# Attention scores of three batches as three rounded products, in four chunks of 112 query rows

## The chip, the cores and the metric

The kernel runs on one core of a Trainium2 chip. The metric is the time of one execution on the device, in microseconds (us). A profiled execution of the same program gives the rows shown below; its times count from the first instruction. Engines: PE is TensorE (matmuls and transposes), DVE is VectorE, ACT is ScalarE, POOL is GpSimd, SP is the engine whose queue issues nearly all transfers.

## The reference

Attention whose heads are mixed before and after the softmax, and then a gated feed-forward layer over all tokens. Batch 4, 12 heads, 448 positions, head size 64; 1792 tokens of 768, hidden size 1536; all in float32.

```python
scores = scale * np.matmul(q, k.transpose(0, 1, 3, 2))
scores = np.einsum('bhij,hg->bgij', scores, w_pre)
scores = scores - np.max(scores, axis=-1, keepdims=True)
attn = np.exp(scores)
attn = attn / (np.sum(attn, axis=-1, keepdims=True) + 1e-09)
attn = np.einsum('bhij,hg->bgij', attn, w_post)
attn_out = np.matmul(attn, v)
g = x @ w_gate            # x: attn_out as 1792 rows of 768
out = (g * sigmoid(g) * (x @ w_val)) @ w_out
```

The change touches the first line alone: the scores of batches 1, 2 and 3.

## The kernel before

**Two stages.** For about the first 410 us the attention of four batches runs, and then the feed-forward layer to the end. The change lies in the first.

**Scores.** q and k are loaded as rows (`load_q`, `load_k`), turned by PE transposes into PSUM (`qprep`: three transposes, half a chunk of queries; `kprep`: four transposes, the keys of a pair of heads), and copied to SBUF (`qcopy` and `kcopy`, tiles `qt` and `kk`). `qk` then multiplies: a group is one pair of heads `p` and one chunk `c` of query rows; head 0 of the pair lies on partitions 0 to 63, head 1 on 64 to 127, so that a group is two products of 64 rows deep, 448 columns wide, one in each half of the array, each into a PSUM bank of its own. Both are float32. `qkcopy` moves the banks to SBUF (`stg`; on ACT or DVE by the parity of the group), and `store` writes them to DRAM (`s_all`), where the scores of all heads of one query row stand together. For batches 1 to 3 chunk 0 has 64 rows (three groups of two pairs, so four products each) and chunks 1 to 3 have 128 (six groups each): 21 groups a batch.

**Steps.** The rest of the attention goes in 23 steps `u` a batch, each of 20 query rows (two tiles of ten). In a step: `gather` reads scores from DRAM (tile `rs`, five buffers, issued two and a half steps ahead), `pre` mixes heads on PE into two PSUM banks, `top` takes row maxima on DVE, `expo` exponentiates on ACT (`e`; reading the banks of `pre` a last time), `norm` and a POOL instruction scale the second mixing's weights, `post` mixes again on PE (for the step before the last two), `mixed` copies that on ACT (`attnT`). In steps 14 to 19 of a batch and 2 to 7 of the next PE also does `av`, attention times values (`values` copies it out); I call these long steps. The others, 8 to 13 and 20 to 1, are short steps. `pre` has two PSUM banks in all, so that `pre` of a step needs that both `expo` of the step before are done.

**Order.** Nothing is scheduled at run time. `at(key, fn)` gives each piece of work a key, and all engines issue by rising key; a step is two units of key long. Within a step `pre` has 0.5, `qk` 0.55, `top` 0.6, `kprep` 0.65, `qprep` 0.66, `qkcopy` 0.7 (1.1 on ACT for even groups), `kcopy` 0.8, `qcopy` 0.81, `expo` 0.95, `post` of an earlier step 1.2, `av` 1.3, `store` 1.4. The scores of a batch are worked out ahead, in steps 14 to 22 of the batch before and 0 to 11 of its own; its k is turned in steps 10 to 15 of the batch before, its chunk 0 of q in steps 11 and 12 there, the halves of chunks 1 to 3 in steps 16, 19, 21 (at its end), 2, 5 and 8. `BACK` sets where this begins.

Of the kernel before, what the change touches and what calls it, by code (L numbers as in the profile page):

```python
# [24 lines left out]
def talking_heads_moe_kernel(ctx, tc, q, k, v, w_pre, w_post, w_gate, w_val, w_out, out):  # L25
# [128 lines left out]
    def scored(c):  # L154
        return P if c else PART

    def row(c):
        return PART + (c - 1) * P if c else 0
# [17 lines left out]
    def load_q(b, c, eng=nc.sync):  # L176
        m = scored(c)
# [1 line left out]
        eng.dma_start(out=qn[b, c][:m], in_=q[b, :, row(c):row(c) + m, :].rearrange("h p d -> p h d"))
# [847 lines left out]
```

## Time and profile before

| | |
|---|---|
| time, median of 3 runs | 944.69 us (943.44 to 947.01) |
| profiled execution, its own time | 941.46 us |
| its span, first to last instruction | 939.7 us |
| mean granted TensorE clock | 0.985 |
| busy over the span | PE 96%, DVE 69%, ACT 46%, POOL 23% |
| the chain that ended last | PE 81%, transfers 9%, DVE 5%, ACT 3% |
| score products (`qk`) on that chain | 6% |

The table's shares are means over two stages that have different limits, so they only say that PE matters most. Matmuls overlap, and a matmul that waits inside the engine counts as busy: whether PE sets the pace in a stretch is read from the order of time there.

### The profile page before, as it was taken

To read this page: it belongs to the slowest core of one execution; us is meant where nothing else is said; L and a number is where in the kernel's file an instruction comes from. 1 tells how busy PE (TensorE), PEld (TensorE's weight loads), DVE (VectorE), ACT (ScalarE), POOL (GpSimd) and SP (SyncE) were. 2 spreads that over 40 slices of the span, in tenths; PEclk is the share of its full clock that TensorE was granted. 3 is DMA by queue.
4 is the path that set the end of the run, shared out by engine and by line. 5 is a ranking of instruction groups with operands and counts; after the bars stand their busy time and mean duration, and the time that the engine had idled before them with its cause. 6 is when DMAs were issued, how large, how long until landed. Compare 5 with 4: busy or idle time off the path is not lost.

```text
span 939.7 us, 27013 instructions
## 1 busy us (share of the span) xinstructions
PE 900.0 (96%) x11276; PEld 717.1 (76%) x11276; DVE 644.0 (69%) x1169; ACT 429.7 (46%) x1006; POOL 219.1 (23%) x291
## 2 busy tenths in 40 slices
PE   8779999899989999899999999999999999999998
PEld 5445655565546565678999999999998999999998
DVE  3556565566655756666999999999849999973210
ACT  2465676567655767553333333333234444431210
POOL 2111111121211111103334443444133332310000
PEclk9799999999989999999999999999999999999999
DMA  8999888998897679523644445476531222211311
GB/s 157 299 284 297 276 285 251 298 290 272 261 324 232 202 273 310 182 95 104 197 152 151 152 151 173 157 268 233 195 113 46 68 68 68 68 51 51 125 40 40
DMA packets 142130, 170.48 MB, mean 181 GB/s; under 512 B 56472, under 2 KB 117432, under 8 KB 142008
## 3 DMA queue, kind: packets, MB, share of 16 engines
q1 hardware_dynamic: 138536, 167.27, 55.9%
q10 hardware_dynamic: 3408, 1.48, 0.8%
q8 instruction: 89, 1.46, 0.7%
q14 instruction: 33, 0.27, 0.1%
q0 software_dynamic: 64, 0.00, 0.0%
HBM read 105.71 MB, written 63.02 MB: 180 GB/s over the span
## 4 chain that ended last, share of the span: by engine, by line
PE 81%; DMA 9%; DVE 5%; ACT 3%; issue 2%; SPq 1%; ACTq 0%; DVEq 0%
PE pre L319 7%; PE av L405 7%; PE dn L842 6%; PE dn L843 6%; PE dn L844 6%; PE post L363 6%; DMA rs<-s_all 6%; PE qk L270 6%; PE p L752 5%; PE p L755 5%; PE p L753 5%; PE upv L808 3%; PE upv L809 3%; PE upv L812 3%; PE upg L812 3%; PE upg L808 3%
## 5 line engine op out<-in xcount | busy, mean ns | idle before, releaser
L336 ACT ACTIVATE e<-pre,st 128x448 f32<-128x448 f32 x180 | 112.6, 630 | 110.8 <-DVE st L330 110.8
L330 DVE TENSOR_REDUCE st<-pre 128x1 f32<-128x448 f32 x180 | 104.0, 618 | 79.2 <-PE pre L319 76.2
L842 PE MATMUL dn<-whi,gh 128*128 128x256 f32 x504 | 141.1, 280 | 1.3 <-DVE u L759 1.3
L844 PE MATMUL dn<-whi,gl 128*128 128x256 f32 x504 | 141.0, 280 | 0.0
L843 PE MATMUL dn<-wlo,gh 128*128 128x256 f32 x504 | 141.0, 280 | 0.0
L347 POOL TENSOR_SCALAR rw<-w_post_gs,st 128x60 f32<-128x60 f32 x180 | 54.3, 317 | 337.9 <-DVE st L344 322.5
L656 POOL TENSOR_SCALAR mag<-mag 128x768 f32<-128x768 f32 x33 | 98.6, 2988 | 145.7 <-ACT mag L654 145.7
L363 PEld LDWEIGHTS post<-rw,e 60*64 60x64 f32 x5040 | 89.5, 138 | 44.9 <-issue 29.7
L319 PE MATMUL pre<-rs,w_pre_blocks 64*64 64x448 f32 (+1 forms) x720 | 103.4, 565 | 21.2 <-DMA rs<-s_all 18.1
L363 PE MATMUL post<-rw,e 60*64 60x60 f32 x5040 | 102.0, 225 | 5.5 <-issue 4.4
L378 ACT ACTIVATE attnT<-post 128x420 f32<-128x420 f32 (+1 forms) x192 | 91.1, 541 | 15.8 <-PE post L363 15.3
L842 PEld LDWEIGHTS dn<-whi,gh 128*128 128x128 f32 x504 | 94.7, 188 | 1.6 <-DVE u L759 1.5
L843 PEld LDWEIGHTS dn<-wlo,gh 128*128 128x128 f32 x504 | 94.7, 188 | 0.0
L844 PEld LDWEIGHTS dn<-whi,gl 128*128 128x128 f32 x504 | 94.7, 188 | 0.0
L405 PE MATMUL av<-attnT,vn 128*64 128x120 f32 (+9 forms) x1728 | 89.4, 262 | 2.7 <-issue 0.9
L270 PE MATMUL qk<-kk,qt 64*128 64x448 f32 (+1 forms) x432 | 88.2, 584 | 0.4 <-DVE qt L248 0.4
L405 PEld LDWEIGHTS av<-attnT,vn 128*64 128x64 f32 (+1 forms) x1728 | 70.8, 136 | 15.3 <-issue 6.4
L279 DVE COPY stg<-qk 128x448 f32<-128x448 f32 x120 | 70.9, 616 | 6.6 <-PE qk L270 6.2
L270 PEld LDWEIGHTS qk<-kk,qt 64*128 64x128 f32 (+1 forms) x432 | 26.9, 165 | 53.7 <-issue 29.7
L684 DVE TENSOR_TENSOR wlo<-w,whi 128x768 fp32r<-128x768 f32 x48 | 45.6, 951 | 29.4 <-ACT whi L688 29.2
L688 ACT ACTIVATE whi<-w 128x768 fp32r<-128x768 f32 x48 | 40.0, 837 | 32.0 <-PE dn L844 21.4
L798 ACT ACTIVATE gh<-m 128x448 fp32r<-128x448 f32 x36 | 20.9, 580 | 71.6 <-DVE m L823 63.4
(120 smaller groups left out, 1672.2 us busy)
## 6 DMA issues: line engine op xcount, KB each, us to landing
rs<-s_all SPq DMA_DIRECT2D x88, 448.0 KB, 5.6
s_all<-stg SPq DMA_DIRECT2D x60, 448.0 KB, 4.9
w_d<-w SPq DMA_DIRECT2D x36, 384.0 KB, 2.7
w<-w_d SPq DMA_DIRECT2D x36, 384.0 KB, 3.4
s_all<-stg SPq DMA_DIRECT2D x45, 224.0 KB, 4.5
raw<-in_moe_w_gate_dram SPq DMA_DIRECT2D x12, 768.0 KB, 4.8
raw<-in_moe_w_val_dram SPq DMA_DIRECT2D x12, 768.0 KB, 6.0
raw<-in_moe_w_out_dram SPq DMA_DIRECT2D x12, 768.0 KB, 5.0
```

The lines of the kernel that those rows point to most:

```text
L270: nc.tensor.matmul(pt[x][i * m:(i + 1) * m], qt[b, c][hs, p, o:o + m], kk[b, p][hs], start=True, stop=True)
L279: nc.vector.tensor_copy(stg[b, c, g][:, x], pt)
L319: nc.tensor.matmul(pt[r][x * HB:(x + 1) * HB], wpre[i], xs[i, x], start=True, stop=True)
L330: nc.vector.tensor_reduce(sts[b, u][:, 0, r:r + 1], pts[b, t], axis=AX.X, op=ALU.max, negate=True)
L336: nc.scalar.activation(e, pts.pop((b, t)), AF.Exp, bias=st[:, 0, r:r + 1], scale=1.0, accum_out=st[:, 1, r:r + 1])
L363: nc.tensor.matmul(ats[b, u][y][o * HB:(o + 1) * HB, to, :m], et[b, t][i, c * P + x * HB:c * P + (x + 1) * HB], rw[b, t][i, :, :m], start= ...
L378: nc.scalar.activation(attnT[:part, i, n0:n1, y * HS:y * HS + m], pt[:part, n0:n1, :m], AF.Copy)
L405: nc.tensor.matmul(o, vn[b][part, h, c], a, start=(c == 0 and x == 0), stop=(c == NC - 1 and x == 2 - m))
L656: eng.tensor_scalar(mag, mag, f32_of(0x38000000), f32_of(0x47EFFFFF), op0=ALU.max, op1=ALU.min)
L842: nc.tensor.matmul(pt, gh, hi, start=opens, stop=False)
L843: nc.tensor.matmul(pt, gh, lo, start=False, stop=False)
L844: nc.tensor.matmul(pt, gl, hi, start=False, stop=closes)
```

## The change

Batches 1 to 3 now split what comes out of the transposes: ACT writes a rounded copy (`hi`, type float32r) and DVE the difference (`lo`, float32r). A score is then three products, hi x hi, hi x lo (k) and lo x hi (q), each one instruction, summed in the same PSUM bank. Chunks have 112 query rows for these batches, so 4 x 6 = 24 groups a batch, each a pair of heads. The keys of a batch are two tiles of all pairs (`xb0`, `xa0` and so on), shared in turn with the tiles of the attention's output. Batch 0 computes as before.

The order moves. `BACK` is 13: everything of a batch's scores begins one step earlier. Groups stand in steps 13 to 22 and 0 to 12, chunk 3 starting one step sooner (`behind` -1), so that step 7 has two groups and every other step one. k is turned in steps 9 to 14, chunk 0 of q in 10 and 11, the other halves in 18, 21, 1, 4, 6 and 9. The diff, cut to its core:

```diff
+    def parted(t, hi, lo):
+        nc.scalar.activation(hi, t, AF.Copy)
+        nc.vector.tensor_tensor(lo, t, hi.bitcast(F32), op=ALU.subtract)
+
     def kcopy(b, p):
-        kk[b, p] = kkp.tile([P, S], F32, tag="kk", name=f"kk_{b}_{p}")
-        if b == 0 and p % 2 == 0:
-            nc.scalar.activation(kk[b, p], trs.pop((b, p)), AF.Copy)
-        else:
-            nc.vector.tensor_copy(kk[b, p], trs.pop((b, p)))
...
+        tr, to = trs.pop((b, p)), [t[:, p] for t in kk[b]]
+        if b:
+            parted(tr, *to)
...
     def qcopy(b, c, g):
-        m = scored(c)
-        nc.vector.tensor_copy(
-            qt[b, c][:, g * (NPAIR // 2):(g + 1) * (NPAIR // 2), :m], qtrs.pop((b, c, g))[:, :, :m]
-        )
+        m = scored(b, c)
+        ps_ = slice(g * (NPAIR // 2), (g + 1) * (NPAIR // 2))
+        tr, to = qtrs.pop((b, c, g))[:, :, :m], [t[:, ps_, :m] for t in qt[b, c]]
+        if b:
+            parted(tr, *to)
+        else:
+            nc.vector.tensor_copy(to[0], tr)
...
-        for i, p in enumerate(pairs):
-            for x in range(2):
-                hs = slice(x * D, (x + 1) * D)
-                nc.tensor.matmul(
-                    pt[x][i * m:(i + 1) * m], qt[b, c][hs, p, o:o + m], kk[b, p][hs], start=True, stop=True
-                )
+        terms = ((0, 0), (0, 1), (1, 0)) if b else ((0, 0),)
+        for j, (u, v) in enumerate(terms):
+            for i, p in enumerate(pairs):
+                for x in range(2):
+                    hs = slice(x * D, (x + 1) * D)
+                    a, w = qt[b, c][u][hs, p, o:o + m], kk[b][v][hs, p]
+                    nc.tensor.matmul(
+                        pt[x][i * m:(i + 1) * m], a, w, start=j == 0, stop=j == len(terms) - 1
+                    )
...
-    BACK = 14
+    BACK = 13
...
-            behind = 0 if b else 2
+            behind = 3 if b == 0 else -1 if c == NC - 1 else 0
```

On PE, in step 10 of batch 1, this stood after `pre` before the change (`qk_1_3_4` is batch 1, chunk 3, pair 4; the last number of a name is its bank or its buffer):

```order
L270 MATMUL qk_1_3_4_0_2731<-kk_1_4_1262,qt_1_3_2337 128x448
L270 MATMUL qk_1_3_4_1_2732<-kk_1_4_1262,qt_1_3_2337 128x448
L224 MATMUL ktr_2_0_2739<-ident_99,kn_2_0_2519 128x128 x3
L224 MATMUL ktr_2_0_2739<-ident_99,kl_2_2517 128x64
L363 MATMUL post_1_8_0_2757<-rw_1_16_2649,e_1_16_2614 64x60 x2
```

and this stands there now (`qt0` is hi of q, `qt1` lo; `kk_1_xb0` is hi of k, `kk_1_xa0` lo):

```order
L285 MATMUL qk_1_3_3_0_2839<-kk_1_xb0_893,qt0_1_3_2495 112x448
L285 MATMUL qk_1_3_3_1_2840<-kk_1_xb0_893,qt0_1_3_2495 112x448
L285 MATMUL qk_1_3_3_0_2839<-kk_1_xa0_894,qt0_1_3_2495 112x448
L285 MATMUL qk_1_3_3_1_2840<-kk_1_xa0_894,qt0_1_3_2495 112x448
L285 MATMUL qk_1_3_3_0_2839<-kk_1_xb0_893,qt1_1_3_2496 112x448
L285 MATMUL qk_1_3_3_1_2840<-kk_1_xb0_893,qt1_1_3_2496 112x448
L220 MATMUL ktr_2_1_2851<-ident_96,kn_2_1_2608 128x128 x3
L220 MATMUL ktr_2_1_2851<-ident_96,kl_2_2502 128x64
L250 MATMUL qtr_2_0_0_2858<-ident_96,qn_2_0_2475 128x112 x3
L379 MATMUL post_1_8_0_2877<-rw_1_16_2739,e_1_16_2705 64x60 x2
```

Six instructions take the place of two (each float32 product runs as two records in the trace), the two halves of the array still alternate, and a `qtr` that stood one step later has come in.

On ACT, in the same step, before the change (`e_1_20` and `e_1_21` are the two exponentials of step 10):

```order
L378 ACTIVATE attnT_109<-post_1_7_0_2685 128x84x5
L378 ACTIVATE attnT_109<-post_1_7_1_2686 128x84x5
L336 ACTIVATE e_1_20_2749,st_1_10_2736<-pre_1_20_2725,st_1_10_2736 128x448
L336 ACTIVATE e_1_21_2753,st_1_10_2736<-pre_1_21_2726,st_1_10_2736 128x448
L281 ACTIVATE stg_1_3_4_2735<-qk_1_3_4_0_2731 128x448
```

and now:

```order
L394 ACTIVATE attnT_106<-post_1_7_1_2794 128x84x5
L224 ACTIVATE kk_1_xb0_893<-ktr_2_1_2851 128x448
L224 ACTIVATE qt0_2_0_2856<-qtr_2_0_0_2858 128x3x112
L352 ACTIVATE e_1_20_2870,st_1_10_2848<-pre_1_20_2833,st_1_10_2848 128x448
L352 ACTIVATE e_1_21_2874,st_1_10_2848<-pre_1_21_2834,st_1_10_2848 128x448
```

The rounded copies of the step's `ktr` and `qtr` now stand ahead of its two exponentials, on an engine where they did not stand at all.

On DVE, again in step 10, before the change (`st` written from `pre` is `top`):

```order
L330 TENSOR_REDUCE st_1_10_2736<-pre_1_21_2726 128x1
L279 COPY stg_1_3_4_2735<-qk_1_3_4_1_2732 128x448
L232 COPY kk_2_0_2747<-ktr_2_0_2739 128x448
L343 TENSOR_SCALAR st_1_10_2736<-st_1_10_2736 128x2
```

and now:

```order
L346 TENSOR_REDUCE st_1_10_2848<-pre_1_21_2834 128x1
L295 COPY stg_1_3_3_2847<-qk_1_3_3_0_2839 112x448
L295 COPY stg_1_3_3_2847<-qk_1_3_3_1_2840 112x448
L225 TENSOR_TENSOR kk_2_2781<-ktr_2_1_2851,kk_1_xb0_893 128x448
L225 TENSOR_TENSOR qt1_2_0_2857<-qtr_2_0_0_2858,qt0_2_0_2856 128x3x112
L359 TENSOR_SCALAR st_1_10_2848<-st_1_10_2848 128x2
```

A subtraction takes the place of a copy and reads what ACT has just written.

## Rows read from the trace of the kernel before

**Rows 1.** Windows: start and end, length, busy us by engine, clock, DMA share, GB/s.

```profile
112.19:127.13 14.94, 14.89 (x319) 7.06 (x312) 10.46 (x25) 10.52 (x29) 2.12 (x7) 1.00 0.66 225
56.37:81.34 24.97, 21.01 (x434) 11.13 (x434) 16.61 (x41) 15.04 (x40) 3.61 (x12) 1.00 1.09 321
155.95:179.51 23.56, 20.34 (x433) 11.01 (x426) 14.88 (x37) 15.29 (x43) 3.61 (x12) 0.93 1.05 318
252.81:277.66 24.85, 20.94 (x434) 11.50 (x426) 15.73 (x43) 15.18 (x42) 4.81 (x15) 0.92 1.09 323
179.51:185.19 5.68, 5.14 (x109) 3.39 (x109) 2.65 (x7) 3.12 (x9) 0.60 (x2) 1.00 0.82 219
277.66:285.34 7.68, 7.68 (x109) 4.62 (x112) 2.65 (x6) 2.90 (x8) 0.60 (x2) 0.60 0.96 301
324.13:351.64 27.51, 27.31 (x606) 17.06 (x610) 17.33 (x54) 18.19 (x60) 4.07 (x14) 1.00 0.79 268
```

**Rows 2.** Timeline of a short step (batch 1, steps 0 and 1): start, length, instructions.

```profile
123.78 0.63 ACT L336 ACTIVATE e<-pre,st 128x448 f32<-128x448 f32 x1
...
125.45 1.02 PE L270 MATMUL qk<-kk,qt 64*128 64x448 f32 x4
125.63 1.16 DVE L330 TENSOR_REDUCE st<-pre 128x1 f32<-128x448 f32 x2 [0.74 <-PE pre L319]
126.35 0.63 ACT L336 ACTIVATE e<-pre,st 128x448 f32<-128x448 f32 x1 [0.53 <-DVE st L330]
...
126.98 0.62 ACT L336 ACTIVATE e<-pre,st 128x448 f32<-128x448 f32 x1
```

**Rows 3.** Timeline of a long step (batch 3, step 6), PE and ACT.

```profile
343.16 0.92 PE L319 MATMUL pre<-rs,w_pre_blocks 60*64 60x448 f32 x8
343.37 0.47 ACT L449 ACTIVATE x<-av 128x100 fp32r<-128x100 f32 x3 [0.95 <-PE av L405]
344.01 1.02 PE L270 MATMUL qk<-kk,qt 64*128 64x448 f32 x4
344.96 1.04 PE L363 MATMUL post<-rw,e 60*64 60x60 f32 x56
347.40 0.92 PE L319 MATMUL pre<-rs,w_pre_blocks 60*64 60x448 f32 x8
```

**Rows 4.** Timeline of PE: a group of four products, and the two passes of a float32 `pre`.

```profile
180.29 0.96 PE L270 MATMUL qk<-kk,qt 64*64 64x448 f32 x8
...
285.34 0.56 PE L319 MATMUL pre<-rs,w_pre_blocks 64*64 64x448 f32 x4
...
285.71 0.56 PE L319 MATMUL pre<-rs,w_pre_blocks 64*64 64x448 f32 x4
```

**Rows 5.** Chain in order of time: six float32r products of the feed-forward layer, 448 columns.

```profile
441.02 1.24 PE upg L812 x6
```

**Rows 6.** Groups by line and shape: busy us, mean ns of one.

```profile
L281 ACT ACTIVATE stg<-qk 128x448 f32<-128x448 f32 x48 | 25.9, 542 | 6.9 <-PE qk L270 6.9
...
L759 DVE TENSOR_TENSOR u<-p,u 128x448 f32<-128x448 f32 x48 | 28.9, 621 | 0.8
```

**Rows 7.** Timeline of PE: transposes of a pair of k, and of half a chunk of q.

```profile
164.08 0.55 PE L224 MATMUL ktr<-ident,kn 128*128 128x128 f32 x3
...
164.55 0.27 PE L224 MATMUL ktr<-ident,kl 64*128 64x64 f32 x1
...
164.75 1.04 PE L363 MATMUL post<-rw,e 60*64 60x60 f32 x56
...
129.60 0.55 PE L241 MATMUL qtr<-ident,qn 128*128 128x128 f32 x3
...
130.08 1.04 PE L363 MATMUL post<-rw,e 60*64 60x60 f32 x56
```

**Rows 8.** The page's transfers: count, size, us from issue to landing.

```profile
rs<-s_all SPq DMA_DIRECT2D x88, 448.0 KB, 5.6
s_all<-stg SPq DMA_DIRECT2D x60, 448.0 KB, 4.9
```

More of the change, by code (lines that the diff above doesn't have):

```diff
@@ L152, in keys, with scored, row @@
         return min(P, S - c * P)
[L154 to L158, printed above, removed]
+    def scored(b, c):
+        return S // NC if b else P if c else PART
+    def row(b, c):
+        return S // NC * c if b else PART + (c - 1) * P if c else 0
     def load_v(b, c):
@@ L176, in load_q @@
     def load_q(b, c, eng=nc.sync):
[L177 removed]
+        m, r = scored(b, c), row(b, c)
         qn[b, c] = nat.tile([P, H, D], F32, tag="qn", name=f"qn_{b}_{c}", bufs=2)
[L179 removed]
+        eng.dma_start(out=qn[b, c][:m], in_=q[b, :, r:r + m, :].rearrange("h p d -> p h d"))
     def load_k(b, p, part=None, eng=nc.sync):
@@ L246, in qcopy @@
     def qcopy(b, c, g):
-        m = scored(c)
-        nc.vector.tensor_copy(
-            qt[b, c][:, g * (NPAIR // 2):(g + 1) * (NPAIR // 2), :m], qtrs.pop((b, c, g))[:, :, :m]
-        )
+        m = scored(b, c)
+        ps_ = slice(g * (NPAIR // 2), (g + 1) * (NPAIR // 2))
+        tr, to = qtrs.pop((b, c, g))[:, :, :m], [t[:, ps_, :m] for t in qt[b, c]]
+        if b:
+            parted(tr, *to)
+        else:
+            nc.vector.tensor_copy(to[0], tr)
     def groups(b, c):
-        if c == 0 or (b == 0 and c < 3):
-            return [(o, (p, p + 1)) for o in range(0, scored(c), PART) for p in range(0, NPAIR, 2)]
+        if b == 0 and c < 3:
+            return [(o, (p, p + 1)) for o in range(0, scored(b, c), PART) for p in range(0, NPAIR, 2)]
         return [(0, (p,)) for p in range(NPAIR)]
@@ L258, in qk @@
         o, pairs = groups(b, c)[g]
-        m = P // len(pairs)
+        m = scored(b, c) if len(pairs) == 1 else PART
         bank = "qk"
@@ L442, in values @@
             return
-        if (0, 0) not in xs_:
-            for x in range(2):
-                xs_[0, x] = stp.tile([P, NKC, TB], F32R, tag="stg", name=f"x{x}")
+        hf = b * S % TB // S
+        if hf not in xs_:
+            n1 = S if hf else NC * SEG
+            xs_[hf] = [stp.tile([P, NKC, n1], F32R, tag=f"x{'ab'[hf]}{x}", name=f"x{hf}{x}") for x in range(2)]
         w = m * SEG if b < B - 1 else n
-        hi, lo = (xs_[0, x][:, p:p + 3 - m, t0:t0 + w] for x in range(2))
+        hi, lo = (xs_[hf][x][:, p:p + 3 - m, t0:t0 + w] for x in range(2))
         for v, h in spread(av, hi):
@@ L704, in x_operands @@
         if i < 2:
-            xw[i] = stp.tile([P, 4, KH, S], F32R, tag="stg", name=f"xw_{i}")
+            ts = [stp.tile([P, 2, KH, S], F32R, tag=f"x{'ab'[i]}{x}", name=f"xw_{i}_{x}") for x in range(2)]
         else:
-            xw[i] = pl["xq"].tile([P, 6, KH, S], F32R, tag="xw", name=f"xw_{i}")
+            t = pl["xq"].tile([P, 6, KH, S], F32R, tag="xw", name=f"xw_{i}")
+            ts = [t[:, 2 * x:2 * x + 2] for x in range(3)]
+        for x, t in enumerate(ts):
+            xw[i, 2 * x], xw[i, 2 * x + 1] = t[:, 0], t[:, 1]
     def x_load(nm):
         i, o = XO[nm]
-        nc.sync.dma_start(out=xw[i][:, o + 1].bitcast(F32), in_=x_o[nm].rearrange("(c p) t -> p c t", p=P))
+        nc.sync.dma_start(out=xw[i, o + 1].bitcast(F32), in_=x_o[nm].rearrange("(c p) t -> p c t", p=P))
     def x_split(nm, low):
         i, o = XO[nm]
-        hi, lo = xw[i][:, o], xw[i][:, o + 1]
+        hi, lo = xw[i, o], xw[i, o + 1]
         if low:
```

51 lines of the change are left out of this document (27 added, 24 removed).

## The prediction

> **What bounds the kernel now.** I read the page for the shares, the windows for the pace of each stretch, the order of time inside a step for what sets it, and the groups for prices. PE's 96% in the table hides three regimes in the 370 us that the change touches.
>
> Long steps are bound by PE. In steps 2 to 7 of batch 3 PE is busy 27.31 of 27.51 us, ACT 18.19, DVE 17.33 [rows 1]. A plain one runs from one `pre` to the next in 4.24 us, with no hole: `pre`, then `qk` from 344.01 to the start of `post` at 344.96, so 0.95 us for a group, then `post` and `av` [rows 3]. PE time saved there is time saved.
>
> Short steps are bound by a loop through three engines, though PE reads as busy (14.89 of 14.94 us [rows 1]). The second `e` of one step ends at 124.41; `qk`, which stands behind `pre` on PE, starts at 125.45; `top` runs from 125.63, the next two `e` from 126.35, and the second ends at 127.60 [rows 2]. So the loop takes 3.2 us: 1.04 from the end of `e` to the start of `qk` (`pre` had to wait for its banks), then 2.15, of which the two `e` are 1.25. `qk` and `post` fit in meanwhile. A shorter `qk` saves nothing here, and anything ahead of `e` on ACT lengthens it.
>
> Steps 8 to 13, in which k of the next batch is turned, go by transfers in batches 0 to 2: 24.97, 23.56 and 24.85 us for six steps, DMA share 1.05 to 1.09, PE with holes (21.01 of 24.97) [rows 1]. Six loops alone would be about 19.
>
> **The change, part by part.**
>
> *The products.* The trace has float32r products of the full depth only: six take 1.24 us, 0.207 each [rows 5]. It has no pair of them in the two halves of the array. A float32 pass of 448 columns takes 0.37 (285.34 to 285.71 [rows 4]), two make 0.75, so 0.95 contains 0.2 of filling and draining. If the halves run beside each other as in float32, a group is 3 x 0.207 + 0.2 = 0.82. Bounds: 0.62 with nothing around the three, 1.44 if the halves take turns (6 x 0.207 + 0.2). I take 0.82, since in float32 four records of a pair overlap in 1.02 us [rows 2]. The group of four products takes 0.96 in the row, 0.89 to the next instruction if its last 0.07 overlap as in [rows 3] (344.01 + 1.02 against 344.96) [rows 4]. So a batch had 18 x 0.95 + 3 x 0.89 = 19.8 us of scores and now has 24 x 0.82 = 19.7: the saved pass is eaten by three more groups. A rule stands beside this: the Trainium skill, FP8 and Floating Point Precision (TensorE Precision Notes), says that true float32 takes four passes; by it three products are three quarters of the time, a rival below. No row here shows four passes as such.
>
> *Long steps, per batch.* Steps 17 to 19 and 2 to 7: nine groups, 0.13 less each, -1.2. Steps 14 to 16: 3 x 0.07, -0.2. The second group of step 7: +0.8. Transposes of q: four halves at 0.48 (129.60 to 130.08 [rows 7]) become three at about 0.42 (112 columns for 128): -0.7. Step 15 loses a pair of k, 0.67 (164.08 to 164.75 [rows 7]): -0.7. Sum -1.9, three times: -5.7. ACT's copy of q does not show: its loop of 4.2 us (below) lies under PE's 4.24 - 0.13 + 0.42.
>
> *The rounded copies on ACT.* This is the costly part. They stand ahead of `e`, and cannot start before the transposes, which stand behind `qk` on PE. From the end of an `e`: 1.04, `qk` 0.82; then for k its transposes 0.8 (164.08 to 164.82, and a hand-over [rows 7]) and the copy of 448 columns, 0.54 [rows 6]; or for q 0.6 and 0.45 (336 columns, between 0.41 by proportion and 0.54); then the two `e` 1.25, and 0.05 for each further hand-over. With k a loop is 4.5, with half a chunk of q 4.2, with both 5.0 (q is ready before k is copied, so it adds 0.45 and a hand-over). Now it is 3.2. That ACT holds a later instruction back while the first waits is not shown by a row; 343.37 shows it idle for 0.95 ahead of a copy whose input was late [rows 3]. The Trainium skill, TensorE: Matmul & The Clock Gate (its section on the 16 sub-arrays), says ACT and DVE are strict first in, first out; by that rule the loops above hold, and the sum is the one below; without it they would stay near 3.2, and the sum would be -6.7. Bounds of the copies: nothing where something else holds the step longer, and 1.0, 1.3 and 1.8 in full.
>
> Steps 21 and 1, once per batch each, had 3.2 and get q: 2 x 1.0 x 3 = +6.0. Step 9 of batch 3 also: +1.0.
>
> Steps 8 to 13 of batches 0 to 2 become 3.2 + 3 x 5.0 + 2 x 4.5 = 27.2 by the loop, against 24.97, 23.56, 24.85 by the transfers: +2.2 +3.6 +2.4 = +8.2. Bounds: 0 if the transfers go on setting the pace, 3 x 8.0 = 24 if the copies add in full.
>
> *DVE.* A subtraction costs what the copy did (621 ns [rows 6]). It waits for ACT, and behind it on DVE stand `norm` and the next `top`; both need the `e` that is late anyway. Nothing more; in long steps `av` waits for a PSUM bank of the turned tile, as now.
>
> *Transfers.* The groups that come to steps 12 and 13 fill holes of PE, but add two stores. Each store has 112 rows for 128, so 392 KB: 784 KB more, 56 KB less in each of steps 8 to 11, and k loads leave one step earlier, 192 KB; net 0.4 MB. The stretch moves 318 GB/s x 23.56 us = 7.5 MB now [rows 1], and 27.2 us have room for 8.6. Hidden; without that room 1.2 us. On SP's queue the last store of chunk 3 stood 1.8 steps ahead of the gather of step 16, and now 0.8, some 3.5 us; a store lands in 4.9 [rows 8], so SP waits about 1.4 us, and the gathers behind it with it. They are issued over two steps ahead of use and land in 5.6 [rows 8]: hidden.
>
> *The clock.* In step 14 of batch 2 the granted clock is 0.60 and the step takes 7.68, against 5.68 at 1.00 in batch 1 [rows 1]: two levels, 1.2 and 2.4 GHz, low after the holes of steps 10 to 13. Groups now fill part of those. Between 0 and -2.0; I take -1.0.
>
> **Sum.** -5.7 +6.0 +1.0 +8.2 -1.0 = +8.5 us. The profiled execution took 941.46 (span 939.7 and 1.8 around it), which makes 950.0; the median of the runs is 944.69, 0.3% above, which makes 953.2.
>
> **Rivals.**
>
> Covered copies: steps 8 to 13 stay with the transfers, term 0. For it: DMA share over 1; two more stores. Against: the loops add to 27.2, and 0.4 MB is 1.2 us. Sum +0.3: 945.
>
> A quarter off (faster): the group is three bare products, 0.62, on the path everywhere, and the copies are covered: 24 x 0.62 = 14.9 for 19.8, -4.9 x 3 = -14.7: 930. This is what the four-pass rule makes of it. For it: PE's 96% and the long steps. Against: the loop of 3.2 us in which `qk` isn't. It decides if a loop with a copy stays under 3.5 us.
>
> Halves in turn: 1.44 a group. Thirteen groups in long steps, 13 x 0.62 x 3 = 24.2, and seven loops with copies a batch, 7 x 0.62 x 3 = 13.0, on top of 8.5: 990. Nothing speaks for it but that the form is not in the trace.
>
> Copies in full: transfers get later as the loops do, and the 24 is paid: -5.7 +6 +1 +24 -1 = +24.3: 969. For it: `pre` waits for gathers and `e` for copies one after the other, and SP waits once more. Against: five gathers are ahead.
>
> **How the numbers follow.** Forecast 0.48, its own range 948 to 959 (the clock term 0 or -2, a group from 0.75 to 0.86). Covered copies 0.22, a quarter off 0.14, halves in turn 0.06, copies in full 0.10. Low 941 (just under covered copies, its clock term at -2 and more) and high 969 hold 0.80. Half a per cent, 4.7 us, is about what a measurement tells from no change. Slower: 0.45 of the forecast, halves, full: 0.61. Same: 0.03 of it and 0.20 of the covered: 0.23. Faster: 0.14 and 0.02: 0.16.
>
> **What would show it.** Right: in steps 9 to 13 `e` idles on ACT behind a copy that waits for `ktr`, steps of 4.5 to 5.0, hardly a wait of `pre` for a gather; steps 21 and 1 of 4.2; plain long steps of 4.1; a group of 0.8 to the next instruction. Wrong: a group of 0.6 or 1.4; steps 9 to 13 of about 4 with `pre` still waiting for gathers; or step 21 still at 3.2, which would mean that the copies are not on the loop.

## The result, and the profile of the changed kernel

The changed kernel takes 951.47 us (median of 7 runs, 948.59 to 954.03), the kernel before, run beside it, 943.79 (7 runs, 942.58 to 947.01). The ratio is 1.0069, with a 95% interval of 1.0047 to 1.0092: slower by 0.7%, 6.5 us. The forecast was 953.2, in a range of 941 to 969. The profiled execution took 952.33 us, its span 950.6, so its trace shows 10.9 us more than that of before: 4.4 us above what the ratio says, since it sets one execution against one.

The page of the changed kernel: busy time, the chain that ended last, and the stores of 112 rows with count, size and us to landing.

```profile
PE 910.7 (96%) x11420; PEld 732.4 (77%) x11420; DVE 654.8 (69%) x1184; ACT 444.3 (47%) x1051; POOL 220.6 (23%) x291
...
PE 80%; DVE 6%; DMA 6%; ACT 5%; issue 3%; SPq 1%; POOL 0%; ACTq 0%; DVEq 0%; POOLq 0%
...
s_all<-stg SPq DMA_DIRECT2D x72, 392.0 KB, 4.7
```

On the page nearly nothing moved: PE is at 96% as before, and transfers went from 9% to 6% of the chain, ACT from 3% to 5%. The 10.9 us have to be looked for by stretches. The windows of the changed kernel, with the columns of [rows 1]: steps 8 to 13 of batches 0, 1 and 2, step 1 of batch 1, step 7 of batch 1, the end of step 7 of batch 2, and steps 8 to 13 and step 15 of batch 3.

```profile
57.45:87.40 29.95, 25.67 (x443) 12.99 (x443) 18.35 (x40) 16.42 (x44) 3.61 (x12) 1.00 1.04 319
161.89:187.00 25.11, 24.00 (x457) 13.27 (x450) 17.47 (x39) 16.68 (x48) 3.01 (x10) 1.00 0.97 309
262.74:288.73 25.99, 24.21 (x458) 13.34 (x450) 18.29 (x45) 16.48 (x46) 3.64 (x11) 1.00 0.99 304
127.95:131.92 3.97, 3.42 (x58) 1.68 (x50) 2.79 (x8) 3.00 (x9) 0.60 (x2) 1.00 0.97 317
155.17:161.89 6.72, 5.59 (x116) 3.60 (x112) 3.08 (x7) 3.94 (x14) 0.98 (x4) 1.00 1.05 262
259.20:262.60 3.40, 3.40 (x72) 3.05 (x66) 0.54 (x3) 1.03 (x3) 0.60 (x2) 0.50 0.92 229
362.39:381.79 19.40, 18.56 (x426) 10.25 (x418) 13.44 (x34) 13.62 (x39) 3.01 (x10) 1.00 0.91 283
386.16:394.46 8.30, 4.42 (x96) 3.19 (x97) 2.34 (x7) 3.60 (x11) 0.75 (x3) 0.87 0.99 344
```

Set against the kernel before by the starts of `pre` (each step from its first `pre` to the next step's), the difference is made of these parts:

| stretch | before | after | difference | forecast |
|---|---|---|---|---|
| up to step 8 of batch 0 | 56.37 | 57.45 | +1.1 | 0 |
| steps 8 to 13, batches 0 to 2 | 24.97, 23.56, 24.85 | 29.95, 25.11, 25.99 | +7.7 | +8.2 |
| steps 20 to 1, three times | 14.94, 15.22, 14.98 | 15.94, 16.12, 16.04 | +3.0 | +6.0 |
| steps 14 to 19, batches 0 to 2 | 30.85, 29.68, 31.49 | 28.58, 28.47, 28.65 | -6.3 | -6.7, both rows and the clock |
| steps 2 to 7, batches 1 to 3 | 28.82, 28.40, 27.51 | 29.97, 31.15, 28.97 | +5.4 | (in the row above) |
| steps 8 to 13 of batch 3 | 19.62 | 19.40 | -0.2 | +1.0 |
| steps 14 to 19 of batch 3 | 28.41 | 30.22 | +1.8 | 0 |
| the rest | | | -1.5 | 0 |

The sum is +10.9, forecast +8.5. Two of its parts were not in the forecast, a wait in steps with two groups and one in step 15 of batch 3. Steps with two groups are step 7 of batches 1 to 3 and also step 13 of batch 0, in which the first group of batch 1 comes on top of one of batch 0. The +7.7 of steps 8 to 13 is +5.0, +1.5 and +1.1 by batch.

The timeline of step 10 of batch 1 (PE, ACT and DVE), which now turns a pair of k and half a chunk of q:

```profile
169.03 1.59 PE L335 MATMUL pre<-rs,w_pre_blocks 64*64 64x448 f32 x8 [0.19 <-ACT e L352]
...
170.56 0.46 PE L285 MATMUL qk<-kk_xb,qt 64*112 64x448 f32 x2
...
170.74 1.15 DVE L346 TENSOR_REDUCE st<-pre 128x1 f32<-128x448 f32 x2 [0.74 <-PE pre L335]
...
170.85 0.36 PE L285 MATMUL qk<-kk_xa,qt 64*112 64x448 f32 x2
171.06 0.37 PE L285 MATMUL qk<-kk_xb,qt 64*112 64x448 f32 x2
171.35 0.55 PE L220 MATMUL ktr<-ident,kn 128*128 128x128 f32 x3
...
172.14 0.54 ACT L224 ACTIVATE kk_xb<-ktr 128x448 fp32r<-128x448 f32 x1 [1.22 <-PE ktr L220]
...
172.58 0.45 ACT L224 ACTIVATE qt<-qtr 128x336 fp32r<-128x336 f32 x1
...
172.93 0.63 ACT L352 ACTIVATE e<-pre,st 128x448 f32<-128x448 f32 x1
...
173.70 1.59 PE L335 MATMUL pre<-rs,w_pre_blocks 64*64 64x448 f32 x8 [0.19 <-ACT e L352]
```

Two things are to be seen. The three pairs of products start 0.29 and 0.21 us apart, and the transposes 0.79 after the first: the halves of the array do run beside each other, and a group costs 0.79 for the 0.95 of [rows 3]. And ACT stands idle for 1.22 us ahead of the rounded copy of k. Both maxima are made by 171.89 (170.74 and 1.15), but `e` starts only at 172.93: it waits behind two copies, `pre` of the next step waits for `e`, and the step takes 4.67 us.

### The profile page after: what moved, and what is told of

It reads as the page before. It is cut to its first block, busy times and chain, and to the rows that moved or that the text cites. A ratio compares the mean times of both kernels' runs of the same rounds, so it can differ in the third digit from the quotient of the medians.

```text
span 950.6 us, 27375 instructions
## 1 busy us (share of the span) xinstructions
PE 910.7 (96%) x11420; PEld 732.4 (77%) x11420; DVE 654.8 (69%) x1184; ACT 444.3 (47%) x1051; POOL 220.6 (23%) x291
## 4 chain that ended last, share of the span: by engine, by line
PE 80%; DVE 6%; DMA 6%; ACT 5%; issue 3%; SPq 1%; POOL 0%; ACTq 0%; DVEq 0%; POOLq 0%
PE pre L335 9%; PE av L421 7%; PE dn L861 6%; PE dn L863 6%; PE dn L862 6%; PE qk L285 6%; PE post L379 5%; PE p L772 5%; PE p L775 5%; PE p L773 5%; PE upv L827 3%; PE upg L827 3%; PE upv L831 3%; PE upv L828 3%; PE upg L828 3%; PE upg L831 3%
## 5 line engine op out<-in xcount | busy, mean ns | idle before, releaser
L335 PE MATMUL pre<-rs,w_pre_blocks 64*64 64x448 f32 (+1 forms) x720 | 115.5, 569 | 17.2 <-ACT e L352 9.4
L379 PEld LDWEIGHTS post<-rw,e 60*64 60x64 f32 x5040 | 87.4, 136 | 26.7 <-issue 18.6
L379 PE MATMUL post<-rw,e 60*64 60x60 f32 x5040 | 99.2, 223 | 1.2 <-ACT attnT L394 1.0
L285 PE MATMUL qk<-kk_xb,qt 64*112 64x448 f32 (+2 forms) x432 | 85.5, 465 | 5.3 <-DVE stg L295 4.6
L285 PEld LDWEIGHTS qk<-kk_xb,qt 64*112 64x112 f32 (+2 forms) x432 | 34.3, 162 | 69.7 <-issue 25.7
L295 DVE COPY stg<-qk 112x448 f32<-112x448 f32 (+1 forms) x135 | 79.6, 615 | 9.6 <-PE qk L285 9.1
L335 PEld LDWEIGHTS pre<-rs,w_pre_blocks 64*64 64x64 f32 (+1 forms) x720 | 28.9, 136 | 41.7 <-ACT e L352 33.6
```

The source lines that it names most:

```text
L285: nc.tensor.matmul(pt[x][i * m:(i + 1) * m], a, w, start=j == 0, stop=j == len(terms) - 1)
L295: nc.vector.tensor_copy(to, pt)
L335: nc.tensor.matmul(pt[r][x * HB:(x + 1) * HB], wpre[i], xs[i, x], start=True, stop=True)
L379: nc.tensor.matmul(ats[b, u][y][o * HB:(o + 1) * HB, to, :m], et[b, t][i, c * P + x * HB:c * P + (x + 1) * HB], rw[b, t][i, :, :m], start= ...
```

## The experiments

Each was compared with runs of the kernel before on the same chip; spans are those of the profiled executions (939.7 before, 950.6 after). A profiled stretch differs between two executions of one order, mostly by when gathers land: the start of step 8 of batch 0, ahead of nearly all edits, lies between 55.1 and 57.7 us. The +1.1 of the table's first row lies inside that. So single steps are read for mechanisms, and the ratios for totals. The diffs are against the changed kernel, the last one against fewer_in_long; they are cut to their core, and `...` marks lines left out.

**late_group.** The second group of a step goes to its end.

```diff
+                y = 0.8 if (b == 1 and c == g == 0) or (b and c == NC - 1 and g == 0) else 0
-                at(n + 0.55, later(qk, b, c, g))
+                at(n + 0.55 + y, later(qk, b, c, g))
-                    at(n + (0.7 if x or g % 2 else 1.1), later(qkcopy, b, c, g, x))
+                    at(n + (1.45 if y else 0.7 if x or g % 2 else 1.1), later(qkcopy, b, c, g, x))
...
```

> The changed kernel, but the second group of step 7 (batches 1 to 3) and of step 13 of batch 0 stands behind post and av on PE, at the end of its step. Theory (the second group waits for the two qk banks until DVE has copied the first group out, which stands behind top; PE's matrices are idle 1.1 to 1.5 us in each of the four): the four steps come down from 6.7 to 8.2 us to about 5.1 (4.27 + 0.8), the clock no longer falls in step 7 of batch 2, total 4.5 to 7 us below the changed kernel, a ratio to the kernel before of about 1.000 to 1.002. Rival (the wait lies beside other waits, and a later group only hands it to the next step): within 1.5 us of the changed kernel.

What it removes is in the timeline of step 7 of batch 1 in the changed kernel:

```profile
156.03 0.46 PE L285 MATMUL qk<-kk_xb,qt 64*112 64x448 f32 x2
156.22 1.16 DVE L346 TENSOR_REDUCE st<-pre 128x1 f32<-128x448 f32 x2 [1.47 <-PE pre L335]
...
157.29 1.15 DVE L295 COPY stg<-qk 112x448 f32<-112x448 f32 x2
...
157.96 0.99 PE L285 MATMUL qk<-kk_xb,qt 64*112 64x448 f32 x2 [1.06 <-DVE stg L295]
```

and what is there instead, in the windows of late_group (step 7 of batches 1, 2 and 3):

```profile
152.35:157.53 5.18, 5.18 (x116) 3.39 (x108) 2.46 (x6) 2.16 (x10) 0.62 (x3) 1.00 0.81 224
250.36:255.35 4.99, 4.99 (x117) 3.27 (x109) 2.87 (x9) 2.04 (x8) 0.69 (x3) 1.00 0.97 267
348.93:353.92 4.99, 4.99 (x117) 3.27 (x109) 2.87 (x9) 2.29 (x9) 1.09 (x4) 1.00 0.73 206
```

A group writes both `qk` banks. The next group of the same step stands directly behind it on PE, but its first bank comes free only when DVE has made `top` and then the copy: 1.06 us of waiting at 157.96. With the group behind `av` the three steps fall from 6.72, 8.22 and 6.92 us to 5.18, 4.99 and 4.99, step 13 of batch 0 from 6.77 to 4.92, and the clock stays at 1.00 in batch 2. Some 2.3 us are given back in step 8 of the three batches, where the loop of the next step starts later. Span 944.9, ratio 1.0023 (1.0001 to 1.0045): 5.7 us below the changed kernel by span, 4.3 by the ratios. The theory holds by the steps and the span; by the ratios the gain is just under its 4.5 to 7.

**copies_behind_e.** The rounded copies follow the exponentials.

```diff
-                at(n + 0.8, later(kcopy, b, p))
+                at(n + 0.99, later(kcopy, b, p))
-                at(n + 0.81 + x, later(qcopy, b, c, g))
+                at(n + (0.81 + x if b == 0 else 1.0), later(qcopy, b, c, g))
```

> The changed kernel, but ACT's rounded copies of k and q for batches 1 to 3 stand behind the two exponentials of their step, and DVE's subtractions follow them there. Theory of the prediction (ACT holds e back while the copy ahead of it waits for the transposes): steps 21 and 1 go from 3.98 back to 3.2 to 3.4 us, six times 0.6 to 0.8 = 3.6 to 4.8 us; steps 8 to 13 of batches 0 to 2 go back to the pace of the transfers, 24 to 25 us (but for the wait of step 13 of batch 0), some 4 to 5 us; total 7 to 10 us below the changed kernel, a ratio of 0.997 to 1.000. Rival (the transfers or the work of ACT as such set these steps; a copy behind e delays the next step instead): within 2 us of the changed kernel.

The timeline of copies_behind_e, in step 10 of batch 1 and then in the long step 4 of batch 1:

```profile
165.67 0.94 PE L335 MATMUL pre<-rs,w_pre_blocks 64*64 64x448 f32 x8
...
167.43 0.64 ACT L352 ACTIVATE e<-pre,st 128x448 f32<-128x448 f32 x1 [0.26 <-DVE st L346]
...
168.67 0.54 ACT L224 ACTIVATE kk_xb<-ktr 128x448 fp32r<-128x448 f32 x1
...
169.31 0.94 PE L335 MATMUL pre<-rs,w_pre_blocks 64*64 64x448 f32 x8
```

```profile
140.00 0.45 ACT L224 ACTIVATE qt<-qtr 128x336 fp32r<-128x336 f32 x1
...
141.04 1.61 PE L421 MATMUL av<-attnT,vn 128*64 128x120 f32 x28 [0.49 <-DVE qt L225]
```

Step 10 goes from 4.67 to 3.64 us with the same instructions, step 1 from 3.97 to 3.26, step 21 from 3.98 to 3.62 (above the 3.2 to 3.4 expected), and steps 8 to 13 of batches 0 to 2 to 27.79, 21.94 and 23.91: 7.4 us won there and 3.2 in steps 21 and 1. That `e` was held by the copies ahead of it is thereby shown; ACT's work is the same. But the long steps 18, 4 and 6 lose 0.3 to 0.85 us each, 6.0 in all: `av` needs both `tr` banks, and the second is held by `qtr` until DVE has subtracted, now behind two exponentials. Span 944.3, ratio 1.0033 (1.0007 to 1.0059): 6.3 us won by span for 7 to 10 expected, 3.4 by the ratios. The mechanism was right, its price in long steps was not foreseen.

**late_magnitudes and loads_behind_gather.** Both move the first feed-forward weights in batch 3: the first moves only ACT's magnitudes (`mag`) and what follows on DVE by a step, the second also the two loads behind the gather of step 16 on SP. The diff is of the second; the first leaves `load_raw` where it stood.

```diff
-                at(START + 0.4 * i if i < 2 else gap(FIRST + 7 * i - 8), later(load_raw, u))
-                at(gap(FIRST + 7 * i - 1, True), later(convert, u, 0))
+                at(START + 1.3 + 0.4 * i if i < 2 else gap(FIRST + 7 * i - 8), later(load_raw, u))
+                at(gap(FIRST + 7 * i - 1 + 2 * (i == 0), True) + 0.1 * (i == 0), later(convert, u, 0))
...
```

> The changed kernel, but the first magnitudes of feed-forward weights on ACT, and the seven conversions that follow on DVE, stand one step later in batch 3. Theory (in step 15 of batch 3 ACT waits 3.73 us for a load that SP could issue only when the last stores of scores had landed, and av waits for ACT): step 15 goes from 8.31 to about 4.7 us, total 3 to 4.5 us below the changed kernel, a ratio of about 1.003. Rival (the conversions are then late for the feed-forward layer, or the load is late for the next step too): within 1 us of the changed kernel.

> The changed kernel, but the first two loads of feed-forward weights stand behind the gather of step 16 of batch 3 on SP's queue, and the first magnitudes one step later and behind ACT's copies of av. Theory (late_magnitudes moved the wait to pre of step 16, whose gather stood behind the two loads, and these waited for the last stores): step 15 of batch 3 comes to about 4.5 us and step 16 to at most 4.7, total 3 to 4 us below the changed kernel, a ratio of about 1.003. Rival (the gather of step 16 itself cannot start before the last stores land, and five gathers and two loads are then moved at once, 3.8 MB): the wait goes to pre of step 16 or 17 again, within 1.5 us of the changed kernel.

The wait in question, in the timeline of step 15 of batch 3 of the changed kernel, with the last store of scores:

```profile
379.33 0.32 SPq L305 DMA_DIRECT2D s_all<-stg  x1
...
385.32 0.37 SPq L654 DMA_DIRECT2D raw<-in_moe_w_gate_dram  x1
...
386.32 2.96 SPq L316 DMA_DIRECT2D rs<-s_all  x5
...
390.17 0.89 ACT L671 ACTIVATE mag<-raw 128x768 f32<-128x768 f32 x1 [3.73 <-DMA raw<-in_moe_w_gate_dram]
...
391.60 2.63 PE L421 MATMUL av<-attnT,vn 128*64 128x120 f32 x32 [3.65 <-DVE x L468]
```

and the same place in late_magnitudes (the wait, and the window of step 16 behind it), then in loads_behind_gather:

```profile
391.52 1.77 PE L335 MATMUL pre<-rs,w_pre_blocks 64*64 64x448 f32 x8 [4.13 <-DMA rs<-s_all]
```

```profile
391.52:397.45 5.93, 5.93 (x98) 4.70 (x101) 1.96 (x5) 2.23 (x6) 0.60 (x2) 0.54 0.44 168
```

```profile
380.46 0.32 SPq L305 DMA_DIRECT2D s_all<-stg  x1
386.80 0.36 SPq L316 DMA_DIRECT2D rs<-s_all  x1
387.21 0.46 SPq L654 DMA_DIRECT2D raw<-in_moe_w_gate_dram  x1
...
394.03 0.90 ACT L671 ACTIVATE mag<-raw 128x768 f32<-128x768 f32 x1 [2.62 <-DMA raw<-in_moe_w_gate_dram]
```

The theory fell both times: spans 948.8 and 948.6, ratios 1.009 (1.0063 to 1.0117) and 1.009 (1.006 to 1.0119), no better than the changed kernel. With the magnitudes later, step 15 takes 7.67 us, since `pre` of step 16 waits for its gather, and step 16 takes 5.93 with PE busy throughout, at a granted clock of 0.54. With the loads behind that gather they take 3.36 and 6.71, since ACT waits again, now ahead of the exponentials of step 16. Steps 14 to 19 are 30.82 and 27.92 us, for 30.23 in the changed kernel: what loads_behind_gather wins there its ratio does not show, and does not exclude. Behind the last store (380.46) SP stands still until it has landed (386.80), and then seven transfers leave at once.

**float32_new_order.** Everything new but the split products: order, 112 rows, pools.

```diff
...
-        terms = ((0, 0), (0, 1), (1, 0)) if b else ((0, 0),)
+        terms = ((0, 0),)
...
-        if b:
-            parted(tr, *to)
-        else:
-            nc.vector.tensor_copy(to[0], tr)
+        nc.vector.tensor_copy(to[0], tr)
```

> The order, chunks and pools of the changed kernel with the products of the kernel before: one float32 product for each head, k and q copied once, on DVE, ahead of nothing on ACT. Theory (the change is two things: products that save about 0.15 us in the 13 groups of long steps of a batch, and a dearer path to them on ACT): against the changed kernel the long steps lose 13 x 0.15 x 3 = 6 us, steps 21 and 1 win 3 to 4 and steps 8 to 13 win 4 to 6; the waits of the second groups and of step 15 of batch 3 stay. In sum 1 to 4 us below the changed kernel, a ratio of 1.003 to 1.006. Rival A (the new order alone is the loss, and the split products cost nothing): the time of the changed kernel plus the 6 us, 1.013. Rival B (the split products are the whole loss): the time of the kernel before, 1.000.

Span 939.3, ratio 0.9989 (0.9964 to 1.0014): the time of the kernel before, rival B's number, and 7.5 us below the changed kernel by the ratios. The steps say why the theory missed. A plain long step is 4.41 us for 4.27, as expected; step 10 of batch 1 is 3.79 for 4.67. Step 7 keeps the wait (6.86, 6.83, 6.77). But the order is worth more than I had counted: steps 14 to 19 of batches 0 to 2 take 28.11, 28.44 and 28.18 us for 30.85, 29.68 and 31.49 before, 7.3 less, with the mean clock at 0.996 for 0.985. So the order's gain and its waits cancel, and the 0.8% lie in the split products and their copies.

**one_product.** Two of the three products are left out (`terms = ((0, 0),)`), with all the copies made, so that it computes the scores from the rounded parts alone.

> The changed kernel without two of the three products (hi x hi alone is computed, the copies are all made), which prices the products where they stand. Theory (a group's products are on the path in long steps, and in steps with copies because the transposes stand behind them): a group of two instructions takes 0.4 for 0.8 us, so a plain long step goes from 4.27 to 3.9, a step with k from 4.32 to 3.9, one with k and q from 4.66 to 4.3, one with q from 3.98 to 3.6; plain short steps stay at 3.20. 21 groups of a batch at 0.4 make 25 us below the changed kernel, a ratio to the kernel before of about 0.98. Rival (in the steps with copies something else, ACT or the transfers, sets the pace): long steps alone, 13 x 0.4 x 3 = 16 us, a ratio of 0.99.

Its windows: step 15 of batch 0 (long, no copy), step 18 (long, q), and step 11 of batch 1 (short, k and q).

```profile
92.70:96.57 3.87, 3.87 (x107) 2.72 (x103) 2.02 (x5) 2.54 (x9) 0.16 (x1) 1.00 0.93 258
104.29:109.46 5.17, 4.52 (x109) 3.00 (x105) 2.87 (x7) 3.48 (x11) 1.05 (x4) 1.00 0.84 261
170.27:174.53 4.26, 4.08 (x74) 2.22 (x74) 3.49 (x9) 3.01 (x9) 0.60 (x2) 1.00 1.05 349
```

A plain long step loses 0.4 (4.27 to 3.87), and so do short steps with copies: 3.98 to 3.57, 4.66 to 4.26, with k alone 4.32 to 3.91; plain short steps stay at 3.20. That confirms that `qk` is on the loop of a short step where transposes stand behind it. But the long steps with copies did not move: 5.17 stays 5.17, 5.02 in batch 2 stays 5.03, 5.94 in step 14 stays 5.94. The products are not what they wait for. The total is ratio 0.9984 (0.9954 to 1.0014), 11.1 us of span where I had 25: four steps a batch do not move, and there are stretches in which the gain is lost again, as step 7 of batch 1 (7.88 us for 6.72, granted clock 0.78).

**both_orders.** late_group, copies behind `e` in short steps alone, and the loads of loads_behind_gather.

```diff
+    SHORT = ((0, 0), (0, 1), (1, 1), (2, 0), (3, 1))
-                at(n + 0.8, later(kcopy, b, p))
+                at(n + (0.99 if p < NPAIR - 1 else 0.8), later(kcopy, b, p))
-                at(n + 0.81 + x, later(qcopy, b, c, g))
+                at(n + (1.0 if b and (c, g) in SHORT else 0.81 + x), later(qcopy, b, c, g))
...
```

> late_group and copies_behind_e together, but the copies stand behind e in short steps alone (steps 9 to 13, 21 and 1); in long steps they stand ahead of e as in the changed kernel. Theory (in copies_behind_e the long steps 4, 6 and 18 lost 0.3 to 0.85 us each, some 6 us, since the turned tile kept a PSUM bank that av waits for; short steps won about 12): 5.7 + 12 = 17 to 18 us below the changed kernel by its span, a ratio to the kernel before of 0.988 to 0.991. Rival (the two gains overlap in steps 8 to 13, where transfers take over): 8 to 11 us below, 0.995 to 0.998.

Span 932.2, 18.4 below the changed kernel; ratio 0.9923 (0.9896 to 0.9951), which by the ratios is 13.8 us. The long steps 4 and 6 of batch 1 are back at 4.71 and 4.71, step 7 is 5.17, step 1 3.27. So the two gains add. This version beats both kernels.

**float32_late.** float32_new_order with the second groups late and the loads behind the gather.

> float32_new_order with the second groups late and the weights' loads behind the gather, as both_orders has them: the products of the kernel before in an order that is equal to that of both_orders but for the copies. Theory (with the copies behind e in short steps the split products are worth what they save in long steps, 13 x 0.14 x 3 = 5.5 us, and the copies in short steps cost nothing or little): the second groups give 5 to 6 us as they did in late_group, so some 934 us of span and a ratio of 0.993, 0 to 6 us above both_orders. Rival (the copies still cost what the products save): 928 or less, below 0.990.

Span 937.7, ratio 0.9965 (0.9945 to 0.9985), 5.5 us of span above both_orders. By steps the split products win 0.14 in each plain long step (4.41 against 4.27, 4.23 against 4.09), and their copies no longer cost anything beside it: step 10 of batch 1 is 3.79 here and 3.73 there, step 21 3.64 and 3.61. The intervals of the two overlap by a little (0.9945 to 0.9951), so the 0.4% between them is likely and not certain. The late groups brought less than in late_group: step 7 went to 5.46, 5.27 and 5.27, 4.5 us in sum, but the span fell by 1.6.

**keys_earlier.** Every pair of k is turned a step earlier, and chunk 3 of batch 3 goes a step earlier, so that steps 6 and 7 there have two groups. The late groups and the copies behind `e` are as in both_orders, its later loads are not in it.

```diff
-                n = slot(BACK - NUB - 4 + p)
+                n = slot(BACK - NUB - 5 + p)
-            behind = 3 if b == 0 else -1 if c == NC - 1 else 0
+            behind = 3 if b == 0 else (-2 if b == B - 1 else -1) if c == NC - 1 else 0
...
```

> both_orders, with every pair of k turned one step earlier (steps 8 to 13, none in the long step 14), and in batch 3 the groups of chunk 3 one step earlier, so that steps 6 and 7 both have two groups and the last store leaves in step 11 as it did in the kernel before. Theory: step 14 goes from 5.9 to about 4.9 in batches 0 to 2 (3 us), step 15 of batch 3 from about 8.3 to 4.7 (3.5 us), step 6 of batch 3 gets 0.8 dearer; some 5.5 us below both_orders, a ratio of 0.982 to 0.986. Rival (step 8 with k costs what step 14 saves; the weights' loads wait elsewhere): within 2 us of both_orders.

Span 935.5, ratio 0.9953 (0.9927 to 0.998): no better than both_orders. Step 14 does fall (4.32, 5.06 and 4.44 for 5.34, 5.51 and 5.33), but waits for transfers take it back: in batch 0 step 8 takes 7.12 us for 4.84, with a wait of `pre` in the timeline of PE in keys_earlier, and step 15 of batch 3 still takes 7.00, though the last store leaves earlier.

```profile
64.79 1.03 PE L335 MATMUL pre<-rs,w_pre_blocks 64*64 64x448 f32 x4 [3.39 <-DMA rs<-s_all]
```

**fewer_in_long.** both_orders, but the last pair of k is turned at the end of step 13, with its copies behind `e` as well, and step 22 has the two groups.

```diff
+                if p == NPAIR - 1:
+                    n = slot(BACK - NUB - 5 + p) + 0.7
...
-            behind = 3 if b == 0 else -1 if c == NC - 1 else 0
-            at_k = [slot(BACK - NUB + done + behind + g) for g in range(len(groups(b, c)))]
+            behind = 3 if b == 0 else -1 if c > 1 else 0
+            at_k = [slot(BACK - NUB + done + behind + g - (b > 0 and c == 1 and g > 3)) for g in range(len(groups(b, c)))]
...
```

> both_orders with two things taken out of long steps: the last pair of k is turned at the end of step 13 in place of step 14, and the step with two groups is 22 (one tile, second group late) in place of 7, chunks 2 and 3 going one step ahead where that follows. Theory (long steps are bound by PE, short ones by the loop, so PE work that moves into a short step is free): step 14 of batches 0 to 2 goes from 5.4 to 4.3 to 4.6, step 7 of batches 1 to 3 from 5.0 to 4.2, steps 13 and 22 get at most 0.4 dearer; in sum 3 to 5 us below both_orders, a ratio of 0.987 to 0.990. Rival (short steps with a second group or a second pair are PE-bound too and pay in full): within 1.5 us of both_orders.

The windows of fewer_in_long: step 22 of batch 0, step 14 of batch 1, steps 14 to 19 of batch 3.

```profile
116.75:120.50 3.75, 3.75 (x86) 2.35 (x77) 2.58 (x8) 2.56 (x9) 0.91 (x3) 1.00 0.98 311
175.84:180.16 4.32, 4.32 (x102) 3.04 (x106) 3.13 (x8) 3.04 (x9) 0.73 (x3) 1.00 0.51 191
362.77:390.22 27.45, 24.33 (x593) 17.68 (x585) 16.14 (x41) 17.22 (x48) 3.03 (x11) 0.94 0.52 177
```

Span 928.2, ratio 0.9887 (0.9864 to 0.991), the best of all: 1.1% under the kernel before. The theory held for the long steps and failed for the short ones. Step 14 is at 4.32 in all three batches, 3.2 us in sum less, but step 13 gives back 1.2, 1.3 and 0, so 2.6 of it. The second group wins 0.9 in step 7 and costs 1.1 in step 22 (2.6 to 3.75): a short step is not free for PE. So these moves explain little of the 4.0 us of span below both_orders. The step from both_orders to here (0.36% with intervals that overlap) is not established by itself; against the kernel before both are.

**magnitudes_two_later.** fewer_in_long, `mag` one more step later.

```diff
-                at(gap(FIRST + 7 * i - 1 + 2 * (i == 0), True) + 0.1 * (i == 0), later(convert, u, 0))
+                at(gap(FIRST + 7 * i - 1 + 4 * (i == 0), True) + 0.1 * (i == 0), later(convert, u, 0))
...
```

> fewer_in_long, with the first magnitudes of feed-forward weights one more step later in batch 3 (at the end of step 16, behind the copies of av), and the conversions on DVE behind them. In loads_behind_gather and fewer_in_long ACT still waits for that load, now ahead of the exponentials of step 16, which takes 6.2 to 6.7 us. Theory (the wait is ACT's, for a load that lands 6 to 7 us after an issue that the last store holds back): step 16 comes to about 4.2 us and steps 14 to 19 of batch 3 from 27.5 to about 25.5, total some 2 us below fewer_in_long, a ratio of about 0.987. Rival (the gathers that are issued in the same burst bind next): pre of step 16 or 17 waits for a gather, and the six steps stay within 0.7 us of 27.5.

In its timeline ACT no longer waits for the load, and `pre` of step 17 waits for a gather that left in the same burst:

```profile
371.68 4.59 SPq L316 DMA_DIRECT2D rs<-s_all  x4
...
378.50 0.90 ACT L675 ACTIVATE mag<-raw 128x768 f32<-128x768 f32 x1
...
381.01 1.77 PE L335 MATMUL pre<-rs,w_pre_blocks 64*64 64x448 f32 x8 [2.85 <-DMA rs<-s_all]
```

The rival's mechanism was right and its size was not: steps 14 to 19 take 29.95 us for 27.45 where it had at most 0.7 more (DVE's conversions now crowd step 19, 7.37 us), ratio 0.9919 (0.9891 to 0.9947). The stretch took 28.41 us in the kernel before, and from 27.2 (keys_earlier) to 32.0 (late_group) in the others. That the transfers which leave once the last store has landed bound it, wherever the weights stand, fits the waits seen, but no run shows it by taking the store or the burst away.

## Why the prediction was right, and where its steps were not

**The costly part was found, and for the stated reason.** "The rounded copies on ACT" had loops of 5.0 (k and q), 4.5 (k) and 4.2 (q); they take 4.66, 4.32 and 3.98. A group is 0.79 and not 0.82, and an instruction on ACT starts 0.10 us before the record of the one ahead ends (172.58 for 172.14 and 0.54), where I had added 0.05 for a hand-over, a figure from no row. The 1.22 us of idle ACT ahead of a copy is the row that was missing before, and copies_behind_e, which changes nothing but the place, brings the loops to 3.64, 3.2 to 4.7 (where gathers then set the pace) and 3.3 to 3.6. The Trainium skill, TensorE: Matmul & The Clock Gate (its section on the 16 sub-arrays), has ACT and DVE as strict first in, first out; the trace agrees, with that 1.22 us. For steps 8 to 13 the sum was +8.2 and came to +7.7, but some 2 us of this are step 13 of batch 0, where two groups stand, which I had not counted, and by batch it was +5.0, +1.5 and +1.1 for +2.2, +3.6 and +2.4. That these offset each other was luck.

**The term for steps 21 and 1 was mis-sized.** I took a loop of 3.2 for both from [rows 2], which are of steps 0 and 1, and added 1.0 six times. Step 1 did go from 3.07, 2.82 and 3.07 to 3.97 each. But step 21 took 3.79 to 3.92 already in the kernel before, and takes 3.98 now. The three steps gave +0.4 for +3.0. The reading of [rows 2] left out that step 21 had a half of q at its end already, and `pre` of step 22 stood behind it, as the kernel before shows in batch 1:

```profile
215.47 0.55 PE L241 MATMUL qtr<-ident,qn 128*128 128x128 f32 x3
...
215.95 0.97 PE L319 MATMUL pre<-rs,w_pre_blocks 64*64 64x448 f32 x4
```

**"The second group of step 7: +0.8" was the step that failed.** It counted the work of PE and not the banks. Step 7 went up by 2.3, 4.0 and 2.7 us (8.9 in sum for the 2.0 of the forecast). The prediction named what is queued behind ACT's copies, but not who must free the two `qk` banks before a group can follow a group. late_group shows it.

**The other long steps won more than forecast,** 9.9 us in the two rows of the table for 8.7, the clock counted in. 0.15 a plain step is right (4.42 to 4.27, 4.24 to 4.09). Step 14 brought most of the surplus: 6.92, 5.67 and 7.68 became 5.94 each. The clock's term of -1.0 had the right sign and was rather too small (0.60 in step 14 of batch 2 became 1.00), but the 6.92 of batch 0 stood at a clock of 1.00. This gain is not the split products': in float32_new_order step 14 takes 5.29, 5.33 and 5.33, so that it belongs to the order. In the changed kernel the split takes 0.6 a step of it back, in both_orders (5.34, 5.51 and 5.33) nearly nothing. "ACT's copy of q does not show" was wrong for batch 2 and step 18: these steps take 4.97 to 5.46 where PE's work makes 4.5 to 4.7, and one_product leaves them where they are. What sets them is the `tr` bank, which I had named ("`av` waits for a PSUM bank of the turned tile, as now") and taken to cost nothing more. In step 18 of batch 1 of the changed kernel DVE's subtraction frees it late, and `av` waits 0.53 us:

```profile
209.22 0.50 DVE L225 TENSOR_TENSOR qt<-qtr,qt 128x336 fp32r<-128x336 f32 x1
...
209.76 1.61 PE L421 MATMUL av<-attnT,vn 128*64 128x120 f32 x28 [0.53 <-DVE qt L225]
```

**"Hidden" was wrong for SP in batch 3.** I had the last store 1.4 us in the way of gathers that have two steps to spare. SP stands for 5.7 us behind it (379.65 to 385.32), and what stands next there is not only a gather but the first two loads of weights, which ACT needs in step 15, where it waits 3.73 us. In sum the stretch got 1.8 dearer. Three attempts to take that wait away moved it to another step.

**The rivals.** "A quarter off" needed a group of 0.62 and covered copies; the group is 0.79 and the copies are not covered. By the four-pass rule that stood beside it (the Trainium skill, FP8 and Floating Point Precision, TensorE Precision Notes) three products would by estimate take 0.71 us for the 0.95; the trace has 0.79, so the measurement decides for less of a gain. "Halves in turn" needed a group of 1.44, and is excluded by the 0.79. "Covered copies" and "copies in full" lie on either side of the +7.7.

So the time came out 1.7 us from the forecast (0.9 of it because the kernel before was that much faster beside the changed one), with errors that offset each other in the traces: +6.9 in step 7 and +1.8 in the last steps of batch 3, against -2.6 in step 21, -1.2 in the other long steps and -1.2 in steps 8 to 13 of batch 3 (there step 9 did get its +1.2, and steps 8 and 13 gave it back). That the loss is there, and why, was argued; that the sum is so close was not.

What stays open: what bounds the last steps of batch 3, and whether the last store there can be made to land sooner, and how much of the 0.4% between both_orders and float32_late is there.

## What to carry to other kernels

An operand that is split on the way to PE is paid at the engine that splits it: before counting passes on PE, look at what stands behind the split's first instruction on its in-order engine, and put it behind what the loop waits for, unless a PSUM bank that PE needs sooner hangs on it. Two groups that share a pool of banks should not stand side by side; at opposite ends of the step the second one costs about its work there (5.18 us for 4.27), though here some 0.8 more in the step behind it. And a change that loses can hide a gain: here the kernel with the same products is 0.7% slower in one order and 0.8 to 1.1% faster in others, of which the order with float32 products (float32_late) has 0.35%.

## What the runs showed of the hardware that was not expected

- Pairs of float32r products of half the depth, in the two halves of the array, start 0.29 and 0.21 us apart at 448 columns (170.56, 170.85 and 171.06); the second interval is what one of full depth takes, 0.207 in [rows 5].
- In step 7 of batch 2, behind the wait for banks, the granted clock fell to 0.50, the lower of its two levels (1.2 of 2.4 GHz), from 259.2 to 262.6 us; PE had been busy for 3.40 of the 4.69 us ahead of it. The step took 8.22 us where the same wait at full clock made 6.72 and 6.92. With the group at the end of the step it stayed at 1.00. In one_product, with fewer products on PE, step 7 of batch 1 had 0.78, for 1.00 in the changed kernel. Behind the waits in batch 3 it fell too: to 0.54 in step 16 of late_magnitudes, with PE busy 3.54 of the 7.67 us of step 15 ahead of it, and step 16 took 5.93 us without a wait.
- The last store of 392 KB in batch 3 holds the next transfer on SP for 5.2 to 7.1 us from its issue (377.05 to 382.27 in late_magnitudes, 379.33 to 385.32 in the changed kernel, 380.46 to 386.80 in loads_behind_gather, 363.12 to 370.18 in magnitudes_two_later), above the page's median of 4.7 from issue to landing.
